# Attention heads regrouped so that 32x32 transpositions on VectorE take the place of 128x128 turns on TensorE

## The chip, the cores and the metric

The kernel runs on one core of a Trainium2 chip. The metric is the device time of one execution in microseconds (us), the median of several runs. The core has a matrix engine (TensorE, "PE" in the profile; "PEld" are its weight loads), a vector engine (VectorE, "DVE"), an activation engine (ScalarE, "ACT"), a general engine (GpSimd, "POOL") and a queue engine that issues transfers (SyncE, "SP"). Each works through its own instructions in order; the engines wait for one another by semaphores. PE writes its results to PSUM, a small memory of banks that DVE and ACT read.

## The reference, cut to what matters

Four layers, A, B, A, B, each added to its input `x` [2048, 512]. The change touches B, an attention with a memory over four segments of 512 rows, with 32 heads of 16 channels:

```python
for s in range(N):                                   # N = 4 segments of L = 512 rows
    qs, ks, vs = q[:, :, s], k[:, :, s], v[:, :, s]
    logits = einsum("bhqd,bhkd->bhqk", qs, ks) * scale + mask
    a_dot = einsum("bhqk,bhkd->bhqd", softmax(logits), vs)
    num = einsum("bhld,bhde->bhle", phi(qs), M)      # reads of the memory
    den = einsum("bhld,bhd->bhl", phi(qs), z) + 1e-6
    outs.append(g * num / den + (1.0 - g) * a_dot)
    M = M + einsum("bhld,bhle->bhde", phi(ks), vs)   # writes to the memory
    z = z + phi(ks).sum over rows
return stack(outs) @ wo
```

Layer A is a linear attention; the change touches it only through the buffers that it shares with B and the function that turns its rows.

## The kernel before

A layer B goes through 32 units `m` = (segment s, chunk c of 8 heads, half of 4 heads). Each m takes five steps, so a segment has 40. The order inside a step is written out by hand in tables: `FIRST` for segment 0, `GAPS` for 1 and 2, `LAST` or `FINAL` for segment 3 of the first or second B layer. A cell "4.1 Q0+/6" is step 1 of the fifth m of the segment (counted from 0), and its words are jobs. This text calls the first step of an m "x.0" and the others x.1 to x.4. Each engine keeps the order in which the program issues its instructions (`Ordered`, `held`).

In every step PE makes products of keys and queries for `attend` (exponentials on ACT, tile `P`, masked on POOL by `affine_select`) and for `maxima` of a later m (row maxima on DVE, "CUSTOM_DVE" in the profile, out of the PSUM tiles `mx`, `my` or two of the four banks `g`). The rest of a step of kind x.1 to x.4 is a projection: Q (queries and keys), V (values), O (output rows), P (output rows of the last segment).

Step x.0 holds the work around the change:

- `weighted(m)`: PE multiplies values and `P`. The result is transposed: for four heads a strip of 32 partitions each (16 channels, then the sum of the weights), with 512 queries along the row. ACT copies it to tile `U`.
- `finish(m)` ("fin"): four transpositions of `U` on PE bring the queries onto the partitions, four heads of 32 columns side by side in a bank `g`. `weigh` has DVE take the reciprocal of the weights' sum and multiply; from segment 1 on POOL adds the product to `sums`, a tile `ot` or `tmp` with a row of 128 channels for each query.
- `reads(s, c)` ("a"): PE multiplies the queries' features (tile `tb`, 128 columns as weights) with the memory `kn` (tile `mem`, 8 heads of 17 columns); `weigh` divides and puts it into `sums`. It has two halves, and in segment 3 and in 1 and 2 they lie in different steps.
- `writes(s, c)` ("m", "t"): four transpositions of the keys' features and 16 small matmuls, 128x32 weights in four column groups with 34 columns on the right side (`g<-v,KN`).
- `turns(s)` ("turn"): for 128 rows, `turn` makes four transpositions of `sums` on PE, a copy `oh` on ACT and the remainder `ol` on DVE; both go into the output projection. `early` ("pre", "pt") does this for three chunks of the last segment, `end_turn` for the fourth.
- `put_maxima(m)` ("max"): PE transposes the maxima into bank `mx`, ACT copies them to `mt`, and a transfer in the next step puts them into the queries' stack.
- "ln": the next segment's normalised rows are turned on PE (`columns`), with a copy `hh` on ACT and a remainder `hl` on DVE.

Layer A turns each 128 rows with the same `turn`; the rows of its last four tiles are kept in `self.rest` and turned by layer B's segment 0.

Of the kernel before, what the change touches and what calls it, by code (L numbers as in the profile page):

```python
# [7 lines left out]
F32 = mybir.dt.float32  # L8
# [8 lines left out]
H = 32  # L17
# [6 lines left out]
PW = 64  # L24
# [3 lines left out]
OT = 6  # L28
TA = 8
OO = 2  # L30
MT = 2
# [29 lines left out]
4.0 max ln ln fin | 4.1 Q0+/6       | 4.2 Q0+/6         | 4.3 Q0+/6 | 4.4 load Q0+/6  # L61
5.0 max t2 fin | 5.1 V+/6           | 5.2 V+/6 n        | 5.3 V+/6 n | 5.4 V+/6 w
6.0 m2 max t3 fin | 6.1 Q1+/6       | 6.2 Q1+/6 n       | 6.3 Q1+/6 n | 6.4 Q1+/6 w
7.0 m3 max a0+ a0+ fin | 7.1 V+/6 w | 7.2 V+/6 n        | 7.3 V+/6 n | 7.4 V+/6 w
"""
GAPS = """
0.0 max a1 a1 fin | 0.1 Q2/6 n        | 0.2 Q2/6 n        | 0.3 Q2/6 n | 0.4 Q2/6
# [9 lines left out]
0.0 max a1 a1 fin | 0.1 Q2/6 n        | 0.2 Q2/6 n        | 0.3 Q2/6 n | 0.4 Q2/6  # L77
# [3 lines left out]
4.0 max ln ln a2 fin a2 | 4.1 v/2      | 4.2 v/2           | 4.3 v/2 | 4.4 v/2  # L81
5.0 max a3 a3 fin | 5.1 v/2           | 5.2 v/2           | 5.3 v/2 | 5.4 v/2
6.0 max fin pre | 6.1 pt pt         | 6.2 P/4           | 6.3 P/9 | 6.4 P/5 v/1
7.0 max pt pt fin | 7.1 P/4           | 7.2 P/5 v/1       | 7.3 P/4 v/1 | 7.4 P/5 v/2
# [5 lines left out]
3.0 max a2 a2 fin | 3.1 O/6           | 3.2 O/6           | 3.3 O/6 | 3.4 O/6  # L90
4.0 max turn turn fin | 4.1 O/6        | 4.2 O/6           | 4.3 O/6 | 4.4 O/6
5.0 max a3 a3 fin | 5.1 O/6           | 5.2 O/6           | 5.3 O/6 | 5.4 O/6
6.0 max fin pre | 6.1 pt pt         | 6.2 P/4           | 6.3 P/9 | 6.4 P/5
7.0 max pt pt fin | 7.1 P/4           | 7.2 P/5           | 7.3 P/4 | 7.4
# [6 lines left out]
def interleave_kernel(ctx, tc, x_in, a_wqkv, a_wphi, a_wo, b_wq, b_wk, b_wv, b_wo, b_beta,  # L101
# [92 lines left out]
    def constants():  # L194
# [9 lines left out]
        for j in range(4):  # L204
            dve.tensor_copy(share[32 * j : 32 * j + 32, :], gates[32 * j : 32 * j + 32, 0, j:H:4])
# [91 lines left out]
    def prepare():  # L297
# [8 lines left out]
        def rows():  # L306

            while jobs and len(asked) < 5:
                src, kc = jobs.pop(0)
                asked.append(T2("ot", OT))  # L310
                sync.dma_start(out=asked[-1], in_=src[kc * P : (kc + 1) * P, :])
            return asked.pop(0)
# [4 lines left out]
        def pieces():  # L317
            for m in range(2):
                for kc in range(NC):
                    tiles = parts()  # L320
                    for e in range(2):
                        for r in range(2):
                            views = [tiles[0].rearrange("p (c f r e d) -> p e r c d f", c=NC, f=2, r=2, e=2)]
# [178 lines left out]
    def out_pair(tiles, xdst, w, soon, w0=0, w1=D):  # L502
# [3 lines left out]
        def side(po, o):  # L506
            return (po[:, 0 : w1 - w0], lambda a, kc: o[a][:, kc * P : (kc + 1) * P],
                    lambda b, kc: w[b][:, kc, w0:w1])
# [134 lines left out]
    class LayerA:  # L643
# [4 lines left out]
        def first(self, hT, vv, upcoming):  # L648

            wph = T2("U", 2)[:, 0 : NC * DH].rearrange("p (c f) -> p c f", c=NC)  # L650
# [58 lines left out]
        def pass1(self, first):  # L709
# [40 lines left out]
            for n, s in enumerate(SEGS):  # L750
# [3 lines left out]
                def kproj(t, e=None):  # L754
# [3 lines left out]
                    pk = T2("U", 2)  # L758
# [148 lines left out]
        def pass2(self):  # L907
# [24 lines left out]
            for i in range(NT):  # L932
# [7 lines left out]
                o = T2("ot", OT) if NT - 4 <= i < NT - 2 else T2("tmp", 2)  # L940
# [39 lines left out]
    class LayerB:  # L980
        def __init__(self, xsrc, xdst, layer):
# [3 lines left out]
            self.later, self.late, self.rows, self.turned = [], [], [], []  # L985
# [97 lines left out]
        def sums(self, s, c):  # L1083

            if (s, c) not in self.ot:
                t = ("ot", OT) if (s * NC + c) % (OT + 2) < OT else ("tmp", 2)
                self.ot[s, c] = T2(*t, shape=(P, 4, P))
            return self.ot[s, c]

        def reads(self, s, c):  # L1090

            kn = self.kn[:, c]
# [467 lines left out]
```

## Time and profile before

| | |
|---|---|
| median of 3 runs | 1358.33 us (1356.58 to 1362.43) |
| profiled execution, first to last instruction | 1355.4 us; what lies around it is not given |
| granted TensorE clock, mean | 0.996 |
| transpositions of U on PE, records | 256 |
| transpositions of `tmp` and `ot` on PE, records | 144 and 112 |
| matmuls of the memory's reads, records | 192 (two for each fp32 matmul) |
| first attention layer, first and last start of the copies U | 299.3 and 693.8 us |
| second attention layer, the same | 961.1 and 1344.8 us |

Times are microseconds unless marked ns. A row of groups gives the line, engine, operation, output tile <- input tiles, shape, count, busy time, the mean ns of one, and the idle time of the engine ahead of it with what ended it. A row of the timeline gives start, length, engine, operation, tiles and count; a bracket at its end is the idle time before it and its releaser. Matmuls overlap on PE, so that the lengths of neighbouring rows add up to more than the distance between their starts.

### The profile page before, as it was taken

The page shows a single profiled execution, that of the slowest core. Times are in us where ns is not written, and L with a number is a line of the kernel's source. Part 1 is how long each engine was busy: PE and PEld are TensorE (multiplying, and loading weights), DVE is VectorE, ACT ScalarE, POOL GpSimd, SP SyncE. Part 2 cuts the span into 40 slices and gives each one's busy share as a digit, 9 for nine tenths or more (in the row PEclk, how much of TensorE's full clock was granted, in tenths as well). Part 3 has the DMA queues.
Part 4 walks back from the last instruction along what each step waited for, and adds up shares of the span by engine and source line. Part 5 has one row for each costly group of instructions (what it writes and reads, how often), then busy time and mean ns, then how long its engine had stood idle before and what let it go on. Part 6 is the DMA issues. An engine that isn't in the chain of part 4 may idle for free.

```text
span 1355.4 us, 36817 instructions
## 1 busy us (share of the span) xinstructions
PE 1315.4 (97%) x14056; PEld 1032.6 (76%) x14056; DVE 1039.5 (77%) x3256; ACT 808.6 (60%) x1205; POOL 695.8 (51%) x1060
## 2 busy tenths in 40 slices
PE   7999989999999999999999998999999999999998
PEld 6888868777777777877768886886777777777765
DVE  4766778777888888888667677787778879878883
ACT  5556345547677677677544433453667866766754
POOL 1668666326447557345324356553355656554442
PEclk9999999999999999999999999999999999999999
DMA  6398447535654545546250103755556554554431
GB/s 205 102 336 276 151 135 234 170 100 138 174 166 131 158 118 134 154 119 184 90 184 33 64 33 126 241 164 134 138 159 175 145 160 105 140 136 103 118 96 63
DMA packets 134401, 196.27 MB, mean 145 GB/s; under 512 B 15441, under 2 KB 61649, under 8 KB 133457
## 3 DMA queue, kind: packets, MB, share of 16 engines
q1 hardware_dynamic: 132256, 193.27, 48.9%
q8 instruction: 112, 1.84, 0.5%
q10 hardware_dynamic: 1968, 0.64, 0.2%
q14 instruction: 65, 0.52, 0.1%
HBM read 101.05 MB, written 39.85 MB: 104 GB/s over the span
## 4 chain that ended last, share of the span: by engine, by line
PE 74%; DVE 10%; ACT 5%; issue 4%; POOL 3%; DMA 3%; SPq 1%; ACTq 0%; DVEq 0%; POOLq 0%
PE g L176 56%; PE lg L176 6%; PE g L180 6%; PE mx L176 3%; ACT P L154 3%; POOL P L154 2%; DVE g L154 2%; PE lg L180 2%; SPq L154 1%; POOL tb L154 1%; PE my L176 1%; DMA x<-x 1%; DVE es L154 1%; PE mx L180 1%; DVE my L154 1%
## 5 line engine op out<-in xcount | busy, mean ns | idle before, releaser
L154 ACT ACTIVATE P<-lg 128x1024 f32<-128x1024 f32 x316 | 325.4, 1030 | 167.1 <-PE lg L176 92.5
L154 POOL TENSOR_SCALAR_AFFINE_SELECT P<-P 128x256 f32<-128x256 f32 (+1 forms) x448 | 193.4, 446 | 283.7 <-ACT P L154 279.1
L154 DVE CUSTOM_DVE_ANT_0 g<-g,mask 128x256 f32<-128x256 f32 (+3 forms) x392 | 191.3, 542 | 8.9 <-PE g L176 8.5
L176 PE MATMUL g<-hh,wqk 64*128 64x512 f32 (+1 forms) x960 | 187.3, 392 | 0.5 <-DMA wqk<-wqk 0.4
L176 PE MATMUL g<-w,oh 64*128 64x512 f32 (+2 forms) x880 | 178.9, 385 | 0.6 <-DVE ol L154 0.6
L154 DVE CUSTOM_DVE_ANT_0 mx<-mx,mask 128x512 f32<-128x512 f32 (+2 forms) x316 | 157.4, 498 | 21.5 <-PE my L176 13.7
L154 DVE CUSTOM_DVE_ANT_0 my<-my,mask 128x512 f32<-128x512 f32 (+2 forms) x316 | 163.3, 517 | 0.0
L176 PE MATMUL g<-P,v 128*32 128x128 f32 (+3 forms) x2064 | 151.6, 433 | 3.6 <-DVE mxs L154 2.5
L176 PE MATMUL lg<-e,e 64*128 64x512 f32 (+1 forms) x1010 | 152.0, 339 | 3.1 <-ACT P L154 3.1
L176 PE MATMUL g<-w,hh 64*128 64x512 f32 (+1 forms) x672 | 143.4, 395 | 2.0 <-ACT w L154 1.3
L154 DVE DVE_READ_ACCUMULATOR2_ANT mxs<- 128x1 f32 x1024 | 142.7, 139 | 0.0
L176 PEld LDWEIGHTS g<-P,v 128*32 128x32 f32 x2064 | 61.5, 109 | 87.3 <-issue 59.2
L176 PEld LDWEIGHTS lg<-e,e 64*128 64x128 f32 x1010 | 102.1, 185 | 32.3 <-issue 11.3
L176 PEld LDWEIGHTS g<-w,oh 64*128 64x128 f32 (+1 forms) x880 | 108.3, 186 | 15.6 <-issue 1.5
L176 PEld LDWEIGHTS g<-hh,wqk 64*128 64x128 f32 (+1 forms) x960 | 106.9, 185 | 16.4 <-PE my L176 1.2
L176 PE MATMUL g<-w,ol 64*128 64x512 f32 (+2 forms) x440 | 116.9, 378 | 0.5 <-DVE ol L154 0.5
L154 POOL TENSOR_SCALAR tb<-tb 128x512 f32<-128x512 f32 x72 | 109.0, 1526 | 16.0 <-ACT tb L154 16.0
L176 PE MATMUL g<-hl,wqk 64*128 64x512 f32 (+1 forms) x480 | 106.8, 390 | 0.2
L154 ACT COPY tb<-g 128x512 f32<-128x512 f32 (+1 forms) x132 | 71.1, 576 | 43.5 <-PE g L176 41.7
L176 PEld LDWEIGHTS g<-w,hh 64*128 64x128 f32 (+1 forms) x672 | 84.4, 188 | 16.1 <-ACT w L154 1.6
L176 PE MATMUL g<-w,hl 64*128 64x512 f32 (+1 forms) x336 | 90.2, 393 | 0.0
L154 DVE TENSOR_REDUCE es<-P 128x64 f32<-128x1024 f32 x64 | 77.3, 1208 | 12.8 <-ACT P L154 12.8
(151 smaller groups left out, 2896.9 us busy)
## 6 DMA issues: line engine op xcount, KB each, us to landing
e<-ta SPq DMA_DIRECT2D x384, 128.0 KB
wqk<-wqk SPq DMA_DIRECT2D x128, 256.0 KB
x<-x SPq DMA_DIRECT2D x48, 256.0 KB
ot<-in SPq DMA_DIRECT2D x26, 256.0 KB
pq<-tb SPq DMA_DIRECT2D x24, 256.0 KB
tb<-pq SPq DMA_DIRECT2D x24, 256.0 KB
x<-xr SPq DMA_DIRECT2D x22, 256.0 KB
xr<-x SPq DMA_DIRECT2D x20, 256.0 KB
```

What stands on the lines that cost most here:

```text
L154: i = f(*a, **k)
L176: return held(nc.tensor.matmul(*a, **k))
L180: return held(nc.tensor.transpose(*a))
```

## The change

Heads are numbered so that half `hf` of a chunk holds the heads 8c + 2j + hf (j = 0 to 3) in place of 8c + 4 hf + j. The strip j of `weighted` and the strip j of `sums` then belong to the same partitions 32j to 32j + 31, and a tile of `sums` has, in strip j, 32 queries on the partitions and for each of 16 blocks of queries the two heads' 16 channels.

- `finish` transposes `U` on DVE in 32x32 blocks into a tile `W` of the same ring; `weigh` reads `W` in SBUF.
- `reads` makes, for each block of 32 queries, four matmuls (one for each column group of 32) with 34 columns.
- `turns` makes no transposition for B. Jobs "cv" (`convert`) transpose a whole tile of `sums` on DVE (512 columns), and in the next step ACT copies the high part and POOL (DVE in the last segment) subtracts the low part. `early` and `end` use these tiles.
- In most cells the reads come ahead of "max" and "fin"; the jobs "pt" go.
- Buffers: `ot` 4 for 6, `oh`/`ol` 4 each for 2, `U` 3 for 2, `mt` 1 for 2, the tag `tmp` goes; the values' rows are 14 columns shorter.

```diff
-PW = 64
+PW = 50
-OT = 6
+OT = 4
-OO = 2
-MT = 2
+OO = 4
+UU = 3
+MT = 1
...
 GAPS = """
-0.0 max a1 a1 fin | 0.1 Q2/6 n        | 0.2 Q2/6 n        | 0.3 Q2/6 n | 0.4 Q2/6
+0.0 a1 a1 max fin | 0.1 Q2/6 n cv3    | 0.2 Q2/6 n        | 0.3 Q2/6 n | 0.4 Q2/6
...
-4.0 max ln ln a2 fin a2 | 4.1 Q0+/6      | 4.2 Q0+/6       | 4.3 Q0+/6 | 4.4 load begin Q0+/6
-5.0 max t2 a3 fin | 5.1 V+/6 | 5.2 V+/6 n N      | 5.3 V+/6 n N | 5.4 V+/6
-6.0 m2 max a3 t3 fin | 6.1 Q1+/6       | 6.2 Q1+/6 n N     | 6.3 Q1+/6 n N | 6.4 Q1+/6
-7.0 m3 max a0+ a0+ fin | 7.1 V+/6      | 7.2 V+/6 n N      | 7.3 V+/6 n N | 7.4 V+/6
+4.0 a2 a2 max ln ln fin | 4.1 Q0+/6 cv0  | 4.2 Q0+/6       | 4.3 Q0+/6 cv1 | 4.4 load begin Q0+/6
+5.0 a3 max t2 fin | 5.1 V+/6 | 5.2 V+/6 n N      | 5.3 V+/6 n N | 5.4 V+/6
+6.0 m2 a3 max t3 fin | 6.1 Q1+/6 cv2   | 6.2 Q1+/6 n N     | 6.3 Q1+/6 n N | 6.4 Q1+/6
+7.0 m3 a0+ a0+ max fin | 7.1 V+/6      | 7.2 V+/6 n N      | 7.3 V+/6 n N | 7.4 V+/6
...
 FINAL = """
-0.0 max a1 a1 fin | 0.1 Q2/6          | 0.2 Q2/6          | 0.3 Q2/6 | 0.4 Q2/6
+0.0 a1 a1 max fin | 0.1 Q2/6 cv3      | 0.2 Q2/6          | 0.3 Q2/6 | 0.4 Q2/6
 1.0 max turn turn fin | 1.1 Q3/6       | 1.2 Q3/6          | 1.3 Q3/6 | 1.4 Q3/6
-2.0 max fin | 2.1 O/6           | 2.2 O/6           | 2.3 O/6 | 2.4 O/6
+2.0 max fin | 2.1 O/6 cv0       | 2.2 O/6           | 2.3 O/6 | 2.4 O/6
...
-6.0 max fin pre | 6.1 pt pt         | 6.2 P/4           | 6.3 P/9 | 6.4 P/5
-7.0 max pt pt fin | 7.1 P/4           | 7.2 P/5           | 7.3 P/4 | 7.4
+6.0 max fin pre | 6.1 cv2         | 6.2 P/4           | 6.3 P/9 | 6.4 P/5
+7.0 max fin | 7.1 P/4           | 7.2 P/5           | 7.3 P/4 | 7.4
...
         def reads(self, s, c):
-            kn = self.kn[:, c]
+            kn = self.kn[:, c].rearrange("p (a j e) -> p a j e", a=2, j=4)
...
-            for a in range(2):
-                pn = PS("g", G)
-                for q in range(2):
-                    mm(pn[:, q * 8 * VW : (q + 1) * 8 * VW],
-                       lhsT=ph[:, (2 * a + q) * P : (2 * a + q + 1) * P], rhs=kn,
-                       start=True, stop=True)
-                weigh(ot[:, 2 * a : 2 * a + 2], pn[:, 0 : 16 * VW].rearrange("p (q h e) -> p q h e", q=2, h=8),
-                      1e-6, False)
+            for half in range(2):
+                pn = PS("g", G)[:, 0 : 16 * VW].rearrange("p (q a e) -> p q a e", q=8, a=2)
+                for q in range(8):
+                    for j in range(4):
+                        at = (8 * half + q) * 32
+                        mm(pn[32 * j : 32 * j + 32, q], lhsT=ph[:, at : at + 32], rhs=kn[:, :, j],
+                           start=True, stop=True, tile_position=(0, 32 * j))
+                weigh(ot[:, 8 * half : 8 * half + 8], pn, 1e-6, False)
                 yield
...
-                            h = c * 8 + hf * 4 + hh
+                            h = c * 8 + 2 * hh + hf
...
             for U in self.U.pop(m):
-                n, pt = U.shape[1] // P, PS("g", G)[:, 0 : U.shape[1]]
-                for t in range(n):
-                    tp(pt[:, t * P : (t + 1) * P], U[:, t * P : (t + 1) * P], ident)
-                weigh(self.sums(s, c).rearrange("p q (h d) -> p q h d", d=DH)[:, q0 : q0 + n, 4 * hf : 4 * hf + 4],
-                      pt.rearrange("p (q h e) -> p q h e", q=n, h=4), 0.0, s > 0,
+                n = U.shape[1] // 32
+                W = T2("U", UU)[:, 0 : 32 * n]
+                dve.transpose(out=W, in_=U)
+                weigh(self.sums(s, c)[:, q0 : q0 + n, hf : hf + 1],
+                      W.rearrange("p (q h e) -> p q h e", q=n, h=1), 0.0, s > 0,
                       dve if m == 8 * NSEG - 1 else pool)
...
+        def turn_sums(self, s, c, tags, src, width=512, at=0):
+            if (s, c) not in self.oT:
+                self.oT[s, c] = [T2(tag, bufs, F32R) for tag, bufs in tags]
+            S = T2(*src)[:, 0:width]
+            dve.transpose(out=S, in_=self.ot[s, c][:, at : at + width])
+            return S, [t[:, at : at + width] for t in self.oT[s, c]]
+        def split_sums(self, S, to, eng):
+            hi, lo = to
+            act.copy(hi, S)
+            eng.tensor_tensor(out=lo, in0=S, in1=hi.bitcast(F32), op=SUB)
+        def convert(self, s, c):
+            tags = [("x", 4)] * 2 if self.thin and s == NSEG - 1 and c < 2 else [("oh", OO), ("ol", OO)]
+            S, to = self.turn_sums(s, c, tags, ("U", UU))
+            eng = dve if s == NSEG - 1 else pool
+            self.at.setdefault(self.k + 1, []).append(lambda: self.split_sums(S, to, eng))
+        def rows_T(self, s, t):
+            return lambda a, kc: self.oT[s, kc][a][:, t * P : (t + 1) * P]
...
         def end_turn(self):
-            last = self.ot.pop((NSEG - 1, NC - 1))
-            return [turn([last[:, t], last[:, t + 1]]) for t in (0, 2)]
+            s, c = NSEG - 1, NC - 1
+            width = 256 if self.thin else 512
+            for at in range(0, 512, width):
+                S, to = self.turn_sums(s, c, [("oh", OO), ("ol", OO)], ("tb3", TB3), width, at)
+                self.split_sums(S, to, dve)
```

More of the change, by code (lines that the diff above doesn't have):

```diff
@@ L309, in rows @@
                 src, kc = jobs.pop(0)
-                asked.append(T2("ot", OT))
+                asked.append(T2(("oh", "ol")[len(jobs) % 2], OO))
                 sync.dma_start(out=asked[-1], in_=src[kc * P : (kc + 1) * P, :])
@@ L939, in pass2 @@
                     exp(self.e[n])
-                o = T2("ot", OT) if NT - 4 <= i < NT - 2 else T2("tmp", 2)
+                o = T2("ot", OT) if NT - 4 <= i else T2("U", UU)
                 if i >= NT - 4:
@@ L984, in __init__ @@
             self.pr, self.at, self.k, self.wo, self.thin = {}, {}, BEGIN, [], False
-            self.later, self.late, self.rows, self.turned = [], [], [], []
+            self.later, self.late, self.rows, self.turned, self.oT = [], [], [], [], {}
         def start(self):
@@ L1272, in turns @@
+        def rows_T(self, s, t):
+            return lambda a, kc: self.oT[s, kc][a][:, t * P : (t + 1) * P]
         def turns(self, s):
             if s < 0:
-                rows = [o.rearrange("p (c x) -> p c x", c=NC) for o in self.layer.rest]
-                blocks, xsrc, i = [[o[:, c] for c in range(NC)] for o in rows], self.layer.xsrc, NT - 4
-            else:
-                ot = [self.ot.pop((s, c)) for c in range(NC)]
-                blocks, xsrc, i = [[o[:, t] for o in ot] for t in range(4)], self.xsrc, 4 * s
+                xsrc, i = self.layer.xsrc, NT - 4
+            else:
+                xsrc, i = self.xsrc, 4 * s
@@ L1280, in turns @@
             for t in range(4):
-                self.turned.append((turn(blocks[t]), residual(xsrc, i + t, ("mmq", 2))))
+                if s < 0:
+                    o = turn([self.layer.rest[t][:, c * P : (c + 1) * P] for c in range(NC)])
+                    lhs = lambda a, kc, o=o: o[a][:, kc * P : (kc + 1) * P]
+                else:
+                    lhs = self.rows_T(s, t)
+                self.turned.append((lhs, residual(xsrc, i + t, ("mmq", 2))))
                 yield
@@ L1296, in early @@
             s = NSEG - 1
-            ot = [self.ot[s, c] for c in range(NC - 1)]
             self.xe = [T2("tb2", TB2) for _ in range(4)]
@@ L1491, in steps @@
                 next(after, None)
-            o = self.end_turn()
+            self.end_turn()
             for _ in early:
```

83 lines of the change are left out of this document (37 added, 46 removed).

## The prediction

> **What bounds the kernel now.** I read the page's busy shares first, then the chain that ended last.
>
> ```profile
> PE 1315.4 (97%) x14056; PEld 1032.6 (76%) x14056; DVE 1039.5 (77%) x3256; ACT 808.6 (60%) x1205; POOL 695.8 (51%) x1060
> PE 74%; DVE 10%; ACT 5%; issue 4%; POOL 3%; DMA 3%; SPq 1%; ACTq 0%; DVEq 0%; POOLq 0%
> ```
>
> TensorE (PE) is busy 97% of the span, and 74% of the chain is its work. VectorE (DVE) is next at 77%. Such averages hide stages, so I asked for windows: one segment of an attention layer in each of the two layers, then four steps of one m. Columns: stretch, its us, busy us (instructions) of PE, PEld, DVE, ACT, POOL, the granted clock, DMA share, GB/s.
>
> ```profile
> 430.00:535.00 105.00, 104.08 (x1173) 82.18 (x1171) 89.05 (x341) 74.38 (x108) 64.11 (x112) 1.00 0.51 136
> 990.00:1095.00 105.00, 104.37 (x1178) 81.95 (x1176) 88.00 (x338) 74.77 (x109) 61.47 (x109) 1.00 0.58 156
> 478.77:486.50 7.73, 7.73 (x79) 6.64 (x79) 7.56 (x31) 6.28 (x10) 4.04 (x7) 1.00 0.29 62
> ```
>
> In an attention segment PE is busy 104 of 105 us at the full granted clock (1.00). So PE's queue sets the time there, and a slot taken out of it shortens the segment, if nothing else takes its place. DVE has 16 us free per segment, but unevenly: in the four steps x.1 to x.4 of this m it is busy 7.56 of 7.73 us.
>
> **Terms 1 and 2: transpositions that leave PE.** Matmuls are pipelined, so the price is not the duration of one but the distance from one group's start to the next one's start. PE's timeline has it:
>
> ```profile
> 412.33 0.60 PE L180 MATMUL g<-ident,ot 128*128 128x128 f32 x4
> 412.77 0.60 PE L180 MATMUL g<-ident,tb 128*128 128x128 f32 x4
> 413.21 0.60 PE L180 MATMUL g<-ident,U 128*128 128x128 f32 x4
> ...
> L180 PE MATMUL g<-ident,U 128*128 128x128 f32 x256 | 39.3, 275 | 2.5 <-ACT U L154 2.5
> L180 PE MATMUL g<-ident,tmp 128*128 128x128 f32 x144 | 22.4, 274 | 1.4 <-POOL tmp L154 1.3
> L180 PE MATMUL g<-ident,ot 128*128 128x128 f32 x112 | 16.9, 275 | 0.0
> ```
>
> Four transpositions take 0.44 us (412.77 to 413.21), so 0.11 us each. `finish` issues all 256 of U: 64 x 0.44 = **28.2 us** go. Of the 256 of `tmp` and `ot`, layer A's twelve turned tiles (12 x 4 x 2 = 96) and its last four rows (4 x 4 x 2 = 32) stay, so 128 go, in `turns`, `early` and `end_turn`: 128 x 0.11 = **14.0 us**. With them go the waits in these rows' last column, 2.5 and 1.3 us; I count **2 us** of these. ScalarE's copies to `oh` are as many as before and read SBUF in place of PSUM; the two forms differ by 0.05 us, on an engine that is busy 74 of 105 us:
>
> ```profile
> L154 ACT CAST ta<-tb 128x512 fp32r<-128x512 f32 x64 | 39.2, 613 | 0.3
> L154 ACT CAST oh<-g 128x512 fp32r<-128x512 f32 (+2 forms) x68 | 36.5, 559 | 27.3 <-PE g L180 26.4
> ```
>
> **Term 3: the reads become small matmuls.** Before: four matmuls per (s, c). After: 16 blocks of 32 queries times 4 column groups, 64 matmuls with a 128x32 weight and 34 columns. The same form stands in `writes`:
>
> ```profile
> 374.76 0.50 PE L176 MATMUL g<-v,KN 128*32 128x34 f32 x32
> 375.19 0.28 PE L180 MATMUL mx<-ident,mxs 128*16 128x128 f32 x1
> 375.30 1.09 PE L176 MATMUL g<-mem,tb 128*128 128x136 f32 x8
> 376.23 0.60 PE L180 MATMUL g<-ident,U 128*128 128x128 f32 x4
> 376.76 0.50 PE L176 MATMUL lg<-e,e 64*128 64x512 f32 x2
> ...
> 116.95 1.27 PE L176 MATMUL my<-v,P 128*32 128x17 f32 x128
> ...
> L176 PE MATMUL g<-mem,tb 128*128 128x136 f32 x192 | 28.4, 283 | 0.8 <-DVE hl L154 0.8
> L176 PE MATMUL g<-KN,P 128*64 128x68 f32 x1024 | 37.4, 226 | 6.6 <-ACT P L154 6.6
> ```
>
> An fp32 matmul is two records. The old reads of one (s, c), 8 records, take 375.30 to 376.23 = 0.93 us. `writes` puts 32 records into 374.76 to 375.19 = 0.43 us, 13.4 ns a record, its four column groups side by side. 128 records make 1.72 us, 0.79 more; 192 / 8 = 24 reads: **19.0 us** come. Ends: 128 records of 17 columns took 1.27 us (+8 us in all), and those of KN,P (two column groups, 68 columns) 37.4 / 1024 = 36.5 ns a record (+90 us). I take 13.4, since shape, column groups and strided right side are the same.
>
> So PE's queue loses 28.2 + 14.0 - 19.0 = 23.2 us net.
>
> **Term 4: DVE takes 98 transpositions** (65 of U, 33 of the sums). No row shows one. Nearest rows:
>
> ```profile
> L154 DVE TENSOR_SCALAR x<-x,st 128x512 f32<-128x512 f32 x2 | 1.0, 542 | 0.0
> L154 DVE BATCH_NORM_STATS2 bs<-x 128x6 f32<-128x512 f32 x64 | 43.4, 678 | 7.9 <-DMA x<-in 7.9
> L154 DVE TENSOR_TENSOR w<-P,w 128x512 fp32r<-128x512 f32 x2 | 2.4, 1220 | 0.0
> L154 DVE TENSOR_TENSOR ol<-g,oh 128x512 fp32r<-128x512 f32 x56 | 37.7, 687 | 44.9 <-ACT oh L154 44.8
> ```
>
> 512 elements cost between 0.54 and 1.22 us; I take 0.68, the one-operand row at one element a cycle. The Trainium skill, "VectorE: DVE Perf Modes", "The three transpose paths", has 311 ns for 128 elements a partition in bf16; carried to 512 elements that is about 0.71 us (an estimate), near the value taken. Per segment: 8 + 4 transpositions, 8.2 us, less four `ol` subtractions that go to POOL (2.7): 89 becomes 94.5 us of about 102. The reciprocal and product of `finish` now read SBUF; I leave their price. DVE stays behind PE on the average. Where it lies:
>
> ```profile
> 451.69 0.28 PE L180 MATMUL mx<-ident,mxs 128*16 128x128 f32 x1
> 451.83 0.69 ACT L154 ACTIVATE U<-g,share 128x512 f32<-128x512 f32 x1 [0.89 <-PE g L176]
> 452.41 0.25 ACT L154 ACTIVATE mt<-mx 16x128 fp32r<-16x128 f32 x1
> 452.91 0.17 DVE L154 TENSOR_SCALAR r<-g 128x16 f32<-128x16 f32 x1 [2.09 <-PE g L176]
> 453.24 0.50 PE L176 MATMUL lg<-e,e 64*128 64x512 f32 x2
> 453.57 0.28 PE L176 MATMUL mx<-e,e 63*128 63x256 f32 x1
> 453.75 0.25 DVE L154 RECIPROCAL r<-g 128x16 f32<-128x16 f32 x1
> ...
> 480.78 0.60 DVE L154 CUSTOM_DVE_ANT_0 mx<-mx,mask 128x384 f32<-128x384 f32 x1
> 482.97 0.28 PE L176 MATMUL mx<-e,e 63*128 63x256 f32 x1
> ```
>
> In step x.0 DVE idles 2.09 us; U is ready at 452.52, and its reciprocal came at 453.75, behind PE's transposition. A DVE transposition at 452.5 fits there: that gap hides it. Without the gap it costs 0.68 of DVE's queue, behind whose head stand the next step's maxima, and behind these PE, which wants the bank back. That reserve is 482.97 - 481.38 = 1.6 us where DVE is fullest. The 32 `cv` transpositions stand in x.1 and x.3, which have no gap; each eats 0.68 of the reserve until x.0. In step 4.0 the reads now go first and the columns' low parts (hl) last, which the Q projection of 4.1 wants: some 0.7 us late, four times. I put **4 us** on these, with 0 and 20 as ends.
>
> **Term 5: the maxima's bank.** PE's `mx` transposition is read by ScalarE (mt, done at 452.66), and step x.1 writes that bank at 453.57, 0.9 us later. The U group stood in this gap. Where nothing else follows `max` (about 23 of 64 steps: x.0 of 0, 7, and most of the last segments) PE reaches the bank 0.11 + 0.5 us after the transposition, mt needs 0.75 to 1.0: 0.15 to 0.4 us late. **5 us** come back; the ends are 0 and 23 x 0.5 = 12.
>
> **Costed at nothing.** The 24 `lo` subtractions on POOL:
>
> ```profile
> L154 POOL TENSOR_TENSOR ta<-ot,ta 128x512 fp32r<-128x512 f32 x12 | 15.4, 1294 | 0.2 <-ACT ta L154 0.2
> ```
>
> 1.3 us each, behind the step's mask select and three steps before the weighted sums want the next ones (x.4 of segment 4: one, but behind it). POOL is busy 64 of 105 us; without that cover a late select holds PE up to 1.3 us, 8 times per layer. `max` moves behind the reads, at most 1.72 us: its row copy on ACT's DMA queue goes out in the next step, four steps ahead of its use; SP's queue keeps its residual loads. One `mt` buffer serves, as the copies are a whole m apart. The last transposition chain swaps two PE for two DVE transpositions: 0 to +0.7 us.
>
> **Sum.** -28.2 - 14.0 + 19.0 - 2 + 4 + 5 = -16.2 us against the profiled span of 1355.4. What lies around that span is not shown; the median of the runs is 2.9 above it, and I carry the difference to it: 1358.3 - 16.2 = **1342 us**. Own range 1332 to 1351 (terms 4 and 5 at nearly nothing, or double with the tail). A difference under 0.5% (6.8 us) can't be told from none here.
>
> **Rivals.** *(a) DVE's lag eats it all.* PE waits for its banks 23 / 64 = 0.36 us per m. For: 7.56 of 7.73 busy in x.1 to x.4. Against: a reserve of 1.6 us, and gaps of 2 us in x.0. Time 1352 to 1364, 15%. *(b) Slower: the transposition is dear.* DVE keeps about 4 us of unavoidable idling per segment (half a us per m until U is there). 86.3 + 12 p + 4 passes the 102 us of PE at p = 1.0, and passes today's 105 at p = 1.22, the highest row. At p = 1.5 it is 108: 8 segments x 3.3 = 26 us longer, 1385. Only rows with a costly second operand lie there: 7%. *(c) Slower: small matmuls don't overlap.* At KN,P's 36.5 ns a read takes 4.7 us: +90 - 42 + 7 = 55 us, 1413; halfway between that and 13.4, at 25 ns, a read takes 3.2 us and the sum is +19, 1377. Against: both the 32 and the 128 records in a row above, at 13.4 and 10 ns: 5%. The Trainium skill, "TensorEngine Tiling (Array Packing)", "Instruction Overhead", says a matmul costs at least some 60 cycles and warns against tiling from a small dimension, as here with 34 columns; its floor at 2.4 GHz would be 25 ns a record (an estimate), the case just priced, and the rows of 10 to 13.4 ns speak against it. *(d) More:* reads at the 10 ns of the 17-column row and nothing for terms 4 and 5: -36, 1322; 8%. That the change leaves the PE work in place is ruled out by the diff: no `tp` of U or of the sums remains.
>
> **How the numbers follow.** Forecast 65%, (a) 15%, (b) 7%, (c) 5%, (d) 8%. The forecast's and (d)'s cases are faster by over 0.5% but for 1% at the edge; (a) lies mostly within: faster 0.72, same 0.15, slower 0.13. From 1330 to 1362 leaves out (b), (c) and most of (d).
>
> **What would show it.** `g<-ident,U` gone, `ident` of `tmp`/`ot` down to 128; the reads' group in 128x34 form with 128 records in about 1.7 us; DVE's transposition near 0.68; PE idle before `mx` behind ACT mt up by about 5 us, before `hl` and the DVE-read banks by about 4; a segment down from 105 to about 103 us. A transposition over 1 us, reads over 2.5 us, or PE's share in the segments falling under 95% would make the prediction wrong.

## The result and the profile after

The changed kernel took **1367.41 us** (median of 8 runs, 1363.37 to 1372.67); the kernel before, run beside it, 1358.57 us (8 runs). The ratio is **1.0061, interval 1.0043 to 1.0079**: slower by 8.8 us, where 16 us less were forecast, and above the range's end of 1362. The profiled execution has a span of 1366.4 us, against 1355.4.

The page of the changed kernel: busy times, then the engines' shares of the chain that ended last.

```profile
PE 1294.7 (95%) x16552; PEld 997.1 (73%) x16552; DVE 1089.9 (80%) x3327; ACT 809.1 (59%) x1202; POOL 738.4 (54%) x1084
...
PE 57%; DVE 25%; issue 6%; ACT 5%; DMA 4%; POOL 2%; SPq 1%; DVEq 0%; ACTq 0%; POOLq 0%
```

TensorE lost 20.7 us of busy time (1315.4 to 1294.7), nearly the 23.2 forecast, and yet the span grew. VectorE rose from 10% of the chain to 25%. The two windows of before, asked again for the changed kernel (columns as before: stretch, length, PE, PEld, DVE, ACT, POOL, clock, DMA share, GB/s):

```profile
430.00:535.00 105.00, 99.96 (x1604) 74.95 (x1599) 94.14 (x340) 73.55 (x107) 69.98 (x110) 1.00 0.49 137
990.00:1095.00 105.00, 100.89 (x1367) 76.30 (x1363) 92.80 (x344) 76.15 (x112) 66.10 (x106) 1.00 0.55 156
```

The clock is still 1.00 there, but TensorE now stands idle 4 to 5 us of 105, where it was idle under 1. VectorE has 94.1 us, close to the forecast 94.5. (A window of 105 us is a little more than a segment: from the copy U of step 4.0 to the same copy one segment later it was 102.4 us before, 438.07 to 540.49, and is 104.4 now, 443.31 to 547.75.) The groups by line, columns as on the page (count, busy us, mean ns of one, idle just before and what ended it):

```profile
L155 DVE STREAM_TRANSPOSE U<-U 128x512 f32<-128x512 f32 (+1 forms) x65 | 45.3, 697 | 33.0 <-ACT U L155 33.0
L155 DVE STREAM_TRANSPOSE U<-ot 128x512 f32<-128x512 f32 x30 | 21.1, 705 | 1.7 <-POOL ot L155 1.7
L155 DVE STREAM_TRANSPOSE tb<-ot 128x256 f32<-128x256 f32 (+1 forms) x3 | 1.6, 528 | 0.0
L177 PE MATMUL g<-mem,tb 128*32 128x34 f32 x3072 | 34.6, 198 | 4.0 <-issue 3.5
L181 PE MATMUL g<-ident,U 128*128 128x128 f32 x96 | 15.0, 280 | 0.0
L181 PE MATMUL g<-ident,ot 128*128 128x128 f32 x32 | 4.5, 272 | 0.0
L177 PE MATMUL g<-P,v 128*32 128x128 f32 (+3 forms) x2064 | 151.7, 433 | 18.6 <-DVE mxs L155 17.8 <-POOL mmq L155 0.6 <-POOL P L155 0.2
```

The planned exchange took place: 98 transpositions on VectorE, 94 of them of 512 columns at 0.70 us (0.68 taken) and four of 256, and 96 + 32 = 128 turns left on TensorE. (The name U in the fifth row is a shared buffer's; these are layer A's.) Two entries are bad news. VectorE waits **33.0 us** in line for ScalarE to hand it U; and the value sums (`g<-P,v`) wait 17.8 us for VectorE to have read the maxima (`mxs`) in their bank, against 2.5 us before:

```profile
L176 PE MATMUL g<-P,v 128*32 128x128 f32 (+3 forms) x2064 | 151.6, 433 | 3.6 <-DVE mxs L154 2.5
```

The view of waits of the changed kernel (us in total, times, longest) shows more victims:

```profile
DVE U L155 <- ACT U L155: 33.0, 28, 3.9
...
PEld lg L177 <- ACT P L155: 21.8, 39, 1.5
...
PE g L177 <- DVE mxs L155: 19.3, 35, 1.0
...
ACT oh L155 <- DVE U L155: 14.3, 22, 1.5
```

The loads' wait for the logits' bank behind ScalarE's exponential was 8.2 us before. ScalarE's row for `oh` shows one way to it: `oh` stands in order behind VectorE's turning, and the exponential stands behind `oh`. It isn't all of it: without any transposition (`no_both`, below) 13.3 of the 21.8 us stay. Two stretches of the timeline show both paths, first steps 4.3 and 4.4 with the turning "cv1", then 6.1 to 7.0 with "cv2" (rows between those shown are left out):

```profile
453.21 0.71 DVE L155 STREAM_TRANSPOSE U<-ot 128x512 f32<-128x512 f32 x1
...
454.54 0.46 DVE L155 CUSTOM_DVE_ANT_0 g<-g,mask 128x256 f32<-128x256 f32 x1
454.92 0.14 DVE L155 DVE_READ_ACCUMULATOR2_ANT mxs<- 128x1 f32 x1
...
455.20 2.36 PE L177 MATMUL g<-P,v 128*32 128x512 f32 x32 [0.41 <-DVE mxs L155]
...
475.67 0.70 DVE L155 STREAM_TRANSPOSE U<-ot 128x512 f32<-128x512 f32 x1
476.41 0.62 ACT L155 CAST oh<-U 128x512 fp32r<-128x512 f32 x1 [0.95 <-DVE U L155]
476.94 1.02 ACT L155 ACTIVATE P<-lg 128x1024 f32<-128x1024 f32 x1
478.01 0.51 PE L177 MATMUL lg<-e,e 64*128 64x256 f32 x4
481.25 2.36 PE L177 MATMUL g<-P,v 128*32 128x512 f32 x32 [0.64 <-DVE mxs L155]
483.70 1.17 PE L177 MATMUL g<-mem,tb 128*32 128x34 f32 x107
486.07 0.38 PE L177 MATMUL g<-mem,tb 128*32 128x34 f32 x20 [1.20 <-issue]
```

At 453.21 VectorE turns sums, 0.71 us; the maxima behind it are read by 455.06, and TensorE starts the value sums at 455.20, 0.41 us late. At 475.67 the turning comes late itself: ScalarE waits 0.95 us for it with its copy, its exponential ends at 477.96, and the next logits go out at 478.01. The last row is a third loss: inside a burst of reads TensorE waits 1.20 us for nothing that the profile shows but the issue of its instructions.

I added up from the traces the time in which neither TensorE nor its weight load is busy, in the two attention stretches (285 to 700 us, and from 945 us on): **11.4 us before, 41.3 us after**. By what had ended just before: 17.7 ScalarE (7.3 of it the logits' bank behind the exponential, 7.0 the value sums' bank behind the copies, 2.0 `mt`, the rest smaller), 14.5 the maxima's banks behind VectorE, 4.1 other work of VectorE (3.6 `hl`), 4.1 nothing that the profile shows (issue), 0.9 POOL. The sum is a lower bound of what TensorE loses: a row lasts longer than the distance to the next one, and a stop counts only from the end of the last row.

### The profile page after: what moved, and what is told of

Read it like the earlier page. It is cut to its first block, busy times and chain, and to the rows that moved or that the text cites. A ratio compares the mean times of both kernels' runs of the same rounds, so it can differ in the third digit from the quotient of the medians.

```text
span 1366.4 us, 41853 instructions
## 1 busy us (share of the span) xinstructions
PE 1294.7 (95%) x16552; PEld 997.1 (73%) x16552; DVE 1089.9 (80%) x3327; ACT 809.1 (59%) x1202; POOL 738.4 (54%) x1084
## 4 chain that ended last, share of the span: by engine, by line
PE 57%; DVE 25%; issue 6%; ACT 5%; DMA 4%; POOL 2%; SPq 1%; DVEq 0%; ACTq 0%; POOLq 0%
PE g L177 46%; DVE g L155 4%; PE lg L177 3%; DVE mx L155 3%; DVE U L155 3%; DVE my L155 2%; DVE mxs L155 2%; PE mx L177 2%; PE g L181 2%; PE lg L181 2%; ACT P L155 2%; DVE ta L155 1%; DVE r L155 1%; DVE hl L155 1%; DVE tb L155 1%
## 5 line engine op out<-in xcount | busy, mean ns | idle before, releaser
L155 POOL TENSOR_SCALAR_AFFINE_SELECT P<-P 128x256 f32<-128x256 f32 (+1 forms) x448 | 204.6, 471 | 218.5 <-ACT P L155 216.3
L177 PE MATMUL g<-hh,wqk 64*128 64x512 f32 (+1 forms) x960 | 181.6, 393 | 0.3
L177 PE MATMUL g<-w,oh 64*128 64x512 f32 (+2 forms) x848 | 171.6, 382 | 2.6 <-ACT oh L155 2.6
L177 PE MATMUL g<-P,v 128*32 128x128 f32 (+3 forms) x2064 | 151.7, 433 | 18.6 <-DVE mxs L155 17.8
L177 PE MATMUL lg<-e,e 64*128 64x512 f32 (+1 forms) x1010 | 149.3, 341 | 11.4 <-ACT P L155 10.5
L177 PEld LDWEIGHTS lg<-e,e 64*128 64x128 f32 x1010 | 97.1, 185 | 47.2 <-ACT P L155 21.8
L177 PEld LDWEIGHTS g<-w,oh 64*128 64x128 f32 (+1 forms) x848 | 104.2, 187 | 16.7 <-ACT oh L155 3.5
L177 PE MATMUL g<-w,ol 64*128 64x512 f32 (+2 forms) x424 | 112.6, 378 | 0.0
L177 PEld LDWEIGHTS g<-hh,wqk 64*128 64x128 f32 (+1 forms) x960 | 97.6, 185 | 19.4 <-ACT hh L155 1.4
L177 PE MATMUL g<-hl,wqk 64*128 64x512 f32 (+1 forms) x480 | 100.8, 392 | 1.6 <-DVE hl L155 1.6
L155 POOL TENSOR_TENSOR ot<-ot,wt 128x256 f32<-128x256 f32 x46 | 34.0, 739 | 121.5 <-DVE wt L155 121.5
L177 PE MATMUL mx<-e,e 63*128 63x384 f32 (+3 forms) x323 | 89.2, 337 | 2.9 <-ACT mt L155 2.0
```

The source lines that it names most:

```text
L155: i = f(*a, **k)
L177: return held(nc.tensor.matmul(*a, **k))
```

## The experiments

Ratios are to the kernel before, run in the same batch. Theory D says that VectorE's lateness ate the gain; the rivals at first were I (the small matmuls) and O (the new order); E, F and G came later. The idle column is the sum just described, for the profiled run of each kernel (before: 11.4); busy times of VectorE stand where a page is used below. The last column is the length of the two attention layers of the profiled run, each from its first to its last copy U (before: 394.5 + 383.7 = 778.2).

```
kernel              us       ratio [interval]           DVE busy  PE idle   layers
changed             1367.41  1.0061 [1.0043, 1.0079]    1089.9    41.3     781.9
no_cv               1356.41  0.9975 [0.9962, 0.9988]              32.3     773.0
no_w                1340.63  0.9864 [0.9843, 0.9886]    1045.8    25.4     760.8
no_both             1337.05  0.9834 [0.9800, 0.9868]    1031.5    23.8     758.5
big_reads           1363.45  1.0036 [1.0024, 1.0048]              41.0     779.4
old_order           1375.96  1.0115 [1.0095, 1.0135]              48.7     792.1
split_later         1366.53  1.0060 [1.0037, 1.0082]              40.2     781.2
fin_later           1400.42  1.0307 [1.0285, 1.0330]              70.2     818.9
before_plus_w       1364.29  1.0038 [1.0024, 1.0052]              16.5     784.2
lo_pool             1350.86  0.9943 [0.9923, 0.9964]    1058.0    33.1     771.2
lo_ln               1352.36  0.9936 [0.9914, 0.9957]              36.1     776.7
lo_ln_split         1349.00  0.9915 [0.9883, 0.9946]    1051.6    32.1     770.6
lo_ln_split_add     1405.16  1.0333 [1.0296, 1.0370]    1039.8    71.7     823.6
```

**no_cv**: the sums' transpositions left out.

```diff
-            S = T2(*src)[:, 0:width]
-            dve.transpose(out=S, in_=self.ot[s, c][:, at : at + width])
+            S = self.ot[s, c][:, at : at + width]
```

> Edit of the changed kernel: the 32 whole-tile transpositions of the sums (cv and the last one) are left out; ACT and POOL split the untransposed tile, so the output rows are not the reference's. Theory D (VectorE is late, and PE waits for the banks it and ACT hold): VectorE does 22 us less, ACT's copy oh no longer waits for it in order, the stalls that follow cv (0.8 us in steps 0.3 and 0.2 to 0.6 in 6.3 and 4.1) go: about 10 us less than the changed kernel, near 1357. Theory I (the small matmuls of the reads cost PE and its instruction supply): no change, within 3 us. Theory O (the new order inside step x.0): no change, within 3 us.

11.7 us less than the changed kernel (0.0086 x 1360): as D had it.

**no_w**: U's transpositions left out; the division takes its divisor from the tile `gates` instead (`weigh` has an argument for it).

```diff
-                W = T2("U", UU)[:, 0 : 32 * n]
-                dve.transpose(out=W, in_=U)
+                W = U
...
-                      dve if m == 8 * NSEG - 1 else pool)
+                      dve if m == 8 * NSEG - 1 else pool, gates[:, 0, 0:n].unsqueeze(2))
```

> Edit of the changed kernel: the 65 transpositions of U on VectorE are left out; weigh reads U untransposed, with another tile's numbers under the division, so the sums are not the reference's. Theory D: VectorE does 45 us less; the weighted sums' waits for a bank (10.5 us in the two attention layers) and half of the exponentials' late banks go: 12 to 16 us less than the changed kernel, 1351 to 1355. Theory I: within 3 us. Theory O: within 3 us.

26.8 us less, nearly twice what D expected. Some 4.6 us of it may be the clock (mean 0.997 over these runs against 0.994; an estimate), but the attention layers too are 21.1 us shorter. The larger part of the loss is in `finish`, where the prediction saw a gap.

**big_reads**: the reads made with 128 columns of weights again, eight records in place of 128.

```diff
...
-                for q in range(8):
-                    for j in range(4):
-                        at = (8 * half + q) * 32
-                        mm(pn[32 * j : 32 * j + 32, q], lhsT=ph[:, at : at + 32], rhs=kn[:, :, j],
-                           start=True, stop=True, tile_position=(0, 32 * j))
+                for q in range(2):
+                    mm(pf[:, q * 8 * VW : (q + 1) * 8 * VW],
+                       lhsT=ph[:, (2 * half + q) * P : (2 * half + q + 1) * P], rhs=self.kn[:, c],
+                       start=True, stop=True)
...
```

> Edit of the changed kernel: the reads are four matmuls of 128 columns per (s, c) again, as before the change; their result lies in the wrong layout, so the sums are not the reference's. Theory I: PE's 12.6 us and the 4 us in which PE waited for instructions go, and VectorE's division starts earlier: about 16 us less than the changed kernel, near 1351. Theory D: PE waits for VectorE's banks anyway, so at most 6 us less. Theory O: about 3 us less, as the reads in front of the maxima become shorter.

Only 3.4 us less, as both D (at most 6) and O (about 3) allow. Theory I falls: the small matmuls cost something, but not the loss.

**old_order**: "max" ahead of the reads again, as in the table of before; of twelve such lines one is shown.

```diff
-4.0 a2 a2 max ln ln fin | 4.1 Q0+/6 cv0  | 4.2 Q0+/6       | 4.3 Q0+/6 cv1 | 4.4 load begin Q0+/6
+4.0 max ln ln a2 fin a2 | 4.1 Q0+/6 cv0  | 4.2 Q0+/6       | 4.3 Q0+/6 cv1 | 4.4 load begin Q0+/6
```

> Edit of the changed kernel: only the order of the jobs in step x.0 is that of before (maxima and normalised rows ahead of the reads, the sums finished between the two halves in 4.0). Theory O: the late low parts in 4.1 (0.77 us, four times), the waits behind mt (2 us) and part of 7.0 go: 6 to 9 us less than the changed kernel. Theory D: within 3 us, VectorE has the same work. Theory I: within 2 us.

7.3 us slower than the changed kernel. O falls with the sign turned: the new order is worth 7 us. D, which allowed 3, missed too. In the trace of `old_order` TensorE stands 4.4 us behind VectorE's division of the reads (`ot`), which there comes late to free its bank `g`; in the changed kernel none of its idle time ends with that division. So the order inside the step counts beside the amount of work.

**before_plus_w**: the kernel before, with 65 transpositions of 256 columns on VectorE whose result nobody reads.

```diff
                 n, pt = U.shape[1] // P, PS("g", G)[:, 0 : U.shape[1]]
+                dve.transpose(out=T2("wt", 1, shape=(P, 256)), in_=U[:, 0:256])
```

> Edit of the kernel before: VectorE makes one more 32x32 transposition of half of U (256 columns, 0.53 us) in every finish, into a tile that nobody reads; 34 us more on VectorE, PE's work untouched. Theory D: 8 to 15 us slower than the kernel before, 1367 to 1374. If VectorE had room (it is busy 89 of 105 us in a segment): within 3 us of the kernel before.

5.2 us: between the two expectations. The work added was less than they had counted:

```profile
L154 DVE STREAM_TRANSPOSE wt<-U 128x256 f32<-128x256 f32 x65 | 28.3, 436 | 15.3 <-ACT U L154 15.2
```

The 0.53 us were the mean of a group with two shapes (the third row of the groups above: two of 256 columns at 0.44 us and one of 512 at 0.71). So 28.3 us cost 5.2. The kernel before did have a reserve.

**no_both**: `no_cv` and `no_w` together.

> Edit of the changed kernel: both kinds of transposition on VectorE are left out (the 32 of the sums and the 65 of U, with another tile's numbers under the division), so the output is not the reference's. What is left of the change is PE's part: the prediction's terms 1 to 3, -23 to -30 us. Theory D: 1328 to 1336, the two single gains (11 and 27 us) nearly added. If PE's part were smaller than its rows say, or the small matmuls or the order of step x.0 cost much by themselves: 1340 or more.

A little above the band's end. Its page's busy line, one window, and one wait:

```profile
PE 1284.4 (96%) x16552; PEld 991.8 (74%) x16552; DVE 1031.5 (77%) x3229; ACT 807.8 (60%) x1202; POOL 730.2 (55%) x1084
```

```profile
430.00:535.00 105.00, 102.34 (x1624) 78.18 (x1622) 89.03 (x342) 75.39 (x109) 71.71 (x119) 1.00 0.50 138
```

```profile
PE g L177 <- DVE mxs L155: 4.3, 11, 0.7
```

With VectorE at the load it had before (89.03 and 89.05 us in this window) the wait for `mxs` falls from 19.3 to 4.3 us, and the kernel takes 23 us less than before. So the 98 transpositions together cost (1.0061 - 0.9834) x 1359 = **31 us**, some 2 us of which may be the clock (see below); in the attention layers of the profiled runs, where these kernels ran at a clock of 1.00 throughout, it is 781.9 - 758.5 = 23.4 us. TensorE's idle sum holds 17.5 of the 31 us (41.3 to 23.8). Divided by the time they hold VectorE (22.7 us for the sums, 45.3 for U), each us of it costs, by the medians and by the attention layers of one profile each:

```
                                                    medians              layers
sums' turning alone (no_w against no_both)           4.1 / 22.7 = 0.18    2.3 / 22.7 = 0.10
28.3 us added to the kernel before                   5.2 / 28.3 = 0.18    6.0 / 28.3 = 0.21
U's turning alone (no_cv against no_both)           19.2 / 45.3 = 0.42   14.5 / 45.3 = 0.32
sums' on top of U's (changed against no_cv)         11.7 / 22.7 = 0.52    8.9 / 22.7 = 0.39
U's on top of the sums' (changed against no_w)      26.8 / 45.3 = 0.59   21.1 / 45.3 = 0.47
```

The first microseconds find room, the later ones less. The medians alone don't secure that: the 4.1 us are uncertain by 5 to 6 us (from the two intervals, an estimate), and `no_w` ran at a higher clock than the others. The layers give the same order, from one profile each.

The idle sum, taken apart as before, shows the way. From the changed kernel to `no_both` the time behind the maxima's banks falls from 14.5 to 2.8 us (2.7 in the kernel before) and that behind ScalarE's copies out of the value sums' bank from 7.0 to 1.0 (0.5 before). The time behind the logits' bank only falls from 7.3 to 5.5 (1.6 before): most of it does not come from the transpositions.

**fin_later**: if the 33 us in which VectorE stands in line for U are the loss (E), then "fin" one step later, when U has long been there, should win them. One of all the x.0 lines is shown.

```diff
-5.0 a3 max t2 fin | 5.1 V+/6 | 5.2 V+/6 n N      | 5.3 V+/6 n N | 5.4 V+/6
+5.0 a3 max t2 | 5.1 fin V+/6 | 5.2 V+/6 n N      | 5.3 V+/6 n N | 5.4 V+/6
```

> Edit of the changed kernel: finish (transposition of U, division) moves from step x.0 to x.1, where U has long been ready. Rival E (VectorE's idle waits for U, 33 us in all): these go, 6 to 15 us less than the changed kernel. Theory D: the same work in a step without a gap, between 3 us less and 5 us more.

33 us slower: both expectations missed. The row of U's turning in the groups of `fin_later`:

```profile
L155 DVE STREAM_TRANSPOSE U<-U 128x512 f32<-128x512 f32 (+1 forms) x65 | 45.3, 698 | 13.5 <-ACT U L155 13.4
```

VectorE's wait went from 33.0 to 13.5 us, as meant, but the 0.70 us then stand in x.1, where VectorE has no gap, and TensorE's idle time rose from 41.3 to 70.2 us, 34.7 of them behind the maxima's banks (14.5 in the changed kernel). So VectorE's waiting time is not the price; what its work pushes back is. The early place in x.0 was the better one.

**split_later**: ScalarE copies the turned sums two steps after the turning, not one.

```diff
-            self.at.setdefault(self.k + 1, []).append(lambda: self.split_sums(S, to, eng))
+            self.at.setdefault(self.k + 2, []).append(lambda: self.split_sums(S, to, eng))
```

> Edit of the changed kernel: ACT's copy oh and the subtraction ol follow their transposition by two steps instead of one. Rival F (ACT, in order, waits with oh for a late VectorE, and the exponentials behind it come late: 7 us of late lg banks): 4 to 7 us less than the changed kernel. Theory D: within 3 us, since the work on VectorE is the same.

No difference, so F (ScalarE's wait for `oh` as a cause of its own) falls as long as VectorE is this full: 1.1 us of idle time less, no more. The idle time behind the logits' bank did fall, from 7.3 to 4.5 us, but other waits took its place.

**lo_pool**: the 64 subtractions that make the low parts of the queries and keys go from VectorE to POOL.

```diff
-                dve.tensor_tensor(out=lo, in0=raw, in1=hi.bitcast(F32), op=SUB)
+                pool.tensor_tensor(out=lo, in0=raw, in1=hi.bitcast(F32), op=SUB)
```

> Edit of the changed kernel: the 64 subtractions that make the queries' and keys' low parts (ta, 0.69 us each on VectorE) go to POOL (about 1.3 us each there). Theory D (VectorE has too much work in the attention layers): 44 us less on VectorE, a gain of 10 to 18 us on the changed kernel, 1349 to 1357, and faster than before. Rival G (another engine in the middle is as full, POOL becomes late with 83 us more): no gain, the masked P comes late and the time stays at 1365 or more. Rival E (VectorE is late because it waits idly for U at the head of its queue, not because it has too much): gain under 5 us.

Faster than both kernels: 16 us less than the changed one. A row of its groups, and the turning "cv3" behind step 0.0 in its timeline (rows between those shown are left out):

```profile
L155 POOL TENSOR_TENSOR ta<-tb,ta 128x512 fp32r<-128x512 f32 x64 | 83.2, 1301 | 22.6 <-ACT ta L155 12.3 <-DMA x<-x 4.7 <-DMA wqk<-wqk 4.7
```

```profile
495.30 0.71 DVE L155 STREAM_TRANSPOSE U<-ot 128x512 f32<-128x512 f32 x1 [0.51 <-POOL ot L155]
496.05 0.62 ACT L155 CAST oh<-U 128x512 fp32r<-128x512 f32 x1 [1.22 <-DVE U L155]
497.29 1.00 ACT L155 ACTIVATE P<-lg 128x1024 f32<-128x1024 f32 x1
498.35 0.51 PE L177 MATMUL lg<-e,e 64*128 64x256 f32 x4 [1.07 <-ACT P L155]
```

At this spot the bound has moved: VectorE waits for POOL's sums (0.51), ScalarE waits for VectorE (1.22), and TensorE 1.07 us for the exponential. Whether VectorE is early here or POOL, with 83 us more to do, is late, these rows don't tell.

**lo_ln** and **lo_ln_split**: `lo_pool`, with "ln" ahead of "fin" in steps 2.0 and 3.0 (two of the five lines are shown); then with the split two steps later as well, against the wait just shown.

```diff
-2.0 m0 max turn t1 fin ln | 2.1 O/6    | 2.2 O/6           | 2.3 O/6 | 2.4 O/6
-3.0 m1 max turn turn fin ln | 3.1 O/6  | 3.2 O/6           | 3.3 O/6 | 3.4 O/6
+2.0 m0 max turn t1 ln fin | 2.1 O/6    | 2.2 O/6           | 2.3 O/6 | 2.4 O/6
+3.0 m1 max turn turn ln fin | 3.1 O/6  | 3.2 O/6           | 3.3 O/6 | 3.4 O/6
```

> Edit of lo_pool: in steps 2.0 and 3.0 the normalised rows (ln) go ahead of fin. Theory D in its fine form (VectorE's order decides who is late: hl behind the transposition of U frees its bank g late, and PE stands 0.55 to 1.1 us in 3.2, six times): 3 to 5 us less than lo_pool, near 1347. If only the amount counts: within 2 us of lo_pool.

> lo_ln, and oh and ol two steps behind their transposition. In lo_pool ACT waits 1.22 us for the transposition with oh at its head and the exponentials come late (PE 1.07 us at 0.3). Rival F in the unloaded kernel: 3 to 5 us less than lo_ln, 1342 to 1345. Theory D alone: within 2 us of lo_ln, as it was in the changed kernel.

The first brings nothing (a miss). The second has the lowest ratio of the versions that still do all the work, 0.9915, or 11.5 us under the kernel before; but its interval overlaps those of `lo_pool` and `lo_ln`, so only the step to POOL is secured.

**lo_ln_split_add**: more in the same direction, the sum of the queries' features on POOL too.

```diff
-                    if m == 1:
-                        pool.tensor_scalar(raw, raw, 0.0, None, op0=MAX)
-                        pool.tensor_tensor(out=e, in0=e, in1=raw, op=ADD)
+                    pool.tensor_scalar(raw, raw, 0.0, None, op0=MAX)
+                    pool.tensor_tensor(out=e, in0=e, in1=raw, op=ADD)
...
-                todo += [features] + [added] * (m == 0)
+                todo += [features]
```

> lo_ln_split, and the queries' feature sum (24 of 0.83 us on VectorE) as two instructions on POOL, 2.8 us there. Theory D: 20 us less on VectorE, 2 to 5 us faster than lo_ln_split. Rival G (POOL is full now, 78 of 105 us and 11 more): masked P comes late, 2 us slower or more.

Rival G, plainly, and theory D missed: 56 us more than `lo_ln_split` in the same batch. The wait of the loads in its view of waits:

```profile
PEld g L177 <- POOL P L155: 75.7, 63, 3.5
```

POOL masks the exponentials that the value sums take; 40.5 of its 71.7 us of idle TensorE come right behind such a mask. POOL's share of the span is only 62%.

## Why the prediction was wrong

The forecast was 16.2 us less and the result 8.8 us more, 25 us apart. Term 4, the price of the transpositions on VectorE, was too small by about that much: 4 us in the sum, about 30 measured. It is the step that failed.

**Terms 1 and 2 held.** The records are gone as counted, and TensorE's busy time fell. **Term 3 was too dear.** From the first record of a read to the next group most reads take 1.25 to 1.28 us, not 1.72 (443.06 to 444.33 in step 4.0, shown below). All 24 take 36.1 us, 4.0 of them idle time inside; less these 4.0 and the 22.3 of before (24 x 0.93), 9.8 us come in place of 19.0. By `big_reads` only 3.4 of them reach the end; that a slot given back helps TensorE little while it waits for VectorE is the likely reason, not a shown one. Without the transpositions the whole rest of the change gains 23.3 us (`no_both`), which is what terms 1 to 3 gave (23.2). That agreement is in part luck: -28.2 - 14.0 + 9.8 is -32.4, and 12.4 us of new idle time (23.8 - 11.4) more than outweigh the 9.1 us that are missing; the new order, POOL's subtractions and term 5 are in it too.

**Term 4 failed, in its size.** It put 4 us on the transpositions, 20 at most; they cost about 30 by the medians, 23.4 in the attention layers alone. Its price of one (0.68; measured 0.70), their number and VectorE's load (94.5; measured 94.1) were about right, and so was the path that it named: VectorE's queue, the maxima, the bank, TensorE (14.5 us of idle time, 2.8 without the transpositions). Three things were missing.

- "That gap hides it" was wrong. In x.0 VectorE does idle, but for what it waits for in order. The timeline of step 4.0 in the changed kernel:

```profile
443.06 1.33 PE L177 MATMUL g<-mem,tb 128*32 128x34 f32 x128
443.31 0.69 ACT L155 ACTIVATE U<-g,share 128x512 f32<-128x512 f32 x1 [0.89 <-PE g L177]
443.88 0.17 DVE L155 TENSOR_SCALAR r<-g 128x16 f32<-128x16 f32 x1 [1.58 <-PE g L177]
...
444.33 0.28 PE L181 MATMUL mx<-ident,mxs 128*16 128x128 f32 x1
...
445.70 1.29 DVE L155 TENSOR_TENSOR hl<-g,hh 128x512 fp32r<-128x512 f32 x2
...
446.90 0.70 DVE L155 STREAM_TRANSPOSE U<-U 128x512 f32<-128x512 f32 x1
447.04 0.50 PE L177 MATMUL g<-hl,wqk 64*128 64x512 f32 x2 [0.26 <-DVE hl L155]
448.34 0.29 DVE L155 CUSTOM_DVE_ANT_0 mx<-mx,mask 128x128 f32<-128x128 f32 x1
```

  It idles 1.58 us until the reads' first half is there. U is ready at 444.00, but the divisions and `hl` stand ahead, and the turning comes at 446.90, with the next maxima behind it. Where "fin" comes first instead, VectorE stands in line for U (33.0 us in all), and everything behind it too.
- "A reserve of 1.6 us" was spent more than once. It was read at one spot of one m, and lateness was taken to end in the next x.0. The steps x.1 to x.4 leave no room to catch up: in the changed kernel VectorE is busy 7.68 us from 447.38 to 455.20 and 8.65 us from 472.50 to 481.25, all but 0.1 us of each, while TensorE is busy 7.41 and 8.01. The prices per us above, which rise from 0.18 to 0.59 (0.10 to 0.47 in the layers), fit lateness that goes on from one m to the next; no run follows it from m to m.
- The path through ScalarE was not in it: `oh` waits for the turning, and what stands behind `oh` on ScalarE waits too. 14.3 of the 41.3 us stand behind the two banks that ScalarE frees. Half of it, the copies out of the value sums' bank, goes with the transpositions (7.0 to 1.0 us); the logits' bank mostly doesn't (7.3 to 5.5), and `split_later`, which takes `oh` out of the exponentials' way, gains nothing. So this path is smaller than the waits make it look.

That `hl` would be late held in kind: TensorE stands 3.6 us behind it (1.0 before), but not as four waits of 0.7 us in 4.1. There are six of 0.2 to 0.35 there, and five of 0.4 to 0.5 in 3.2, which the prediction did not have.

**Term 5**: about 2 us (the idle time behind `mt`), not 5. **Costed at nothing**: POOL's 24 subtractions indeed held nothing up (0.9 us of idle time behind POOL). Not seen at all: 4.1 us in which TensorE stands idle for nothing that the profile shows, most of it in the bursts of reads. **The segment**, forecast to go down from 105 to about 103 us, was read off a window of 105; by the copies U it went up, from 102.4 to 104.4.

**Rivals.** (a) was the right one, "DVE's lag eats it all", and too mild: it had 0.36 us per m, and the runs show 31 / 64 = 0.48. It also ended at 1364, since it took the lag only to even out the gain; so the mechanism stood in the prediction, but mostly under "same". (b) falls with 0.70 us, (c) with about 10 ns a record. The mark that it set, TensorE's share of the segments under 95%, was just missed: 95.2% and 96.1%.

**What the attention layers don't hold.** In the profiled pair they are longer by 1.6 and 2.1 us. The other 7.3 of the 11.0 us lie outside them, in the layers A and at the edges of B (584.5 us against 577.2). The change reaches the layers A through shared buffers and the turning of their rows; that is not the reason, since `no_both`, with the same layers A, spends 577.4 us outside. In the changed kernel more stretches there had a lower clock. Two windows of the changed kernel, then of the kernel before:

```profile
183.00:188.00 5.00, 4.15 (x45) 3.68 (x45) 4.31 (x10) 2.46 (x3) 3.96 (x5) 0.66 0.01 2
275.00:281.00 6.00, 6.00 (x22) 3.91 (x23) 5.86 (x20) 0.00 (x0) 3.35 (x3) 0.72 0.00 0
```

```profile
183.00:188.00 5.00, 4.67 (x51) 4.02 (x52) 3.20 (x9) 1.83 (x3) 3.94 (x4) 1.00 0.02 5
275.00:281.00 6.00, 6.00 (x61) 4.52 (x60) 5.61 (x24) 1.60 (x2) 4.01 (x3) 1.00 0.33 87
```

The changed kernel spent 20.5 us at half clock, in six stretches of 3.413 us, the kernel before 10.2 in three, mostly at other places. `no_both` had 17.1 us, so the clock does not explain all of the outside either. Over the runs the mean granted clock was 0.9936 against 0.9962 (15 runs of the kernel before, of the first batch of experiments), which by itself makes some 0.26% or 3.5 of the 8.8 us (an estimate). Runs of the changed kernel at 0.996 to 0.997 took 1363.4, still 4.8 us more than the kernel before. Why its clock was lower was not tried and stays open.

## What to carry to other kernels

Work that moves to the second-busiest engine is priced by that engine's slack step by step, in the order of its queue, and not by its average or by an idle gap whose end is set by something else; here the first us cost about 0.2 each and the last 0.5 to 0.6. Where such an engine has no room, make it with the move: sending 64 subtractions on to a third engine turned +0.6% into -0.6%, and one step further cost 4%. Leaving the moved work out (`no_both`) shows in one run what the move is worth if it were free.

## What was not expected of the hardware

- VectorE's transposition of 32x32 blocks in fp32 takes 0.70 us for 512 columns and 0.44 for 256. The estimate of 0.71 from the Trainium skill, "VectorE: DVE Perf Modes", "The three transpose paths", agrees; no run here has its bf16 form.
- 128 records of small matmuls (32 columns of weights, 34 of data, four column groups in turn) take 1.26 us of TensorE's queue as a rule, 9.8 ns a record, under the 13.4 of the 32 in a row; but in such a burst TensorE can stand idle with no releaser in the profile, once for 1.20 us.
- The same subtraction of 128x512 takes 1.30 us on POOL and 0.69 on VectorE.
- In stretches of 3.413 us, one to six in a profiled run (its last microseconds aside), the granted clock was half; some 0.3% of the time hangs on them (the estimate above). Ahead of each, or of the first where several follow one another, TensorE had been busy 2.8 us or less in 3.4. The reverse does not hold: in the kernel before it was busy 1.59 us from 180.0 to 183.4, and the clock behind was 1.00.
